# Second layer's first product by a seven-product scheme inside each block of tokens

## The chip, the cores and the metric

The kernel runs on one core of a Trainium2 chip. The metric is the device time of one execution in microseconds (us). A core has a matrix engine (TensorE, PE in the profile), three engines for elementwise work (VectorE or DVE, ScalarE or ACT, GpSimd or POOL), and a queue on SyncE (SP) from which this kernel issues all of its DMA transfers. Each engine executes its instructions in the order in which the program lists them, and waits for others by semaphores. SBUF is the working memory of 128 partitions; matmuls write into PSUM, which has eight banks of 512 float32 columns.

## The reference

Three stages follow each other; d is 512 wide, tokens are 8 x 576 = 4608.

```python
q_s = softmax(q, axis=-1); k_s = softmax(k, axis=2)
x = q_s @ (k_s^T @ v)                                   # linear attention, 8 heads of 64
x = (sigmoid(x @ w_gate) * (x @ w_val)) @ w_out         # first layer, d_ff = 1536
h = x @ w_in                                            # second layer, d_ff = 2048
P = a0 + a1*h + a2*h**2 + a3*h**3
Q = 1 + |b0|*|h| + |b1|*h**2
out = (P / (Q + 1e-6)) @ w_out2
```

Inputs of the layers' weights are 64-bit floats in the original layout, which the kernel reads as words and turns into float32 ("pieces").

## The kernel before, in words

Tokens are worked on in nine blocks of 512 columns, features in groups of 128 (f). To keep float32 precision at the matrix engine's faster rate every operand is split into a high and a low part (h, lo), and each product of two 128x128 by 128x512 tiles is three matmuls: high by high, low by high, high by low (`mm3`, lines 182 to 185). A split is two operations: ScalarE copies the value to the rounded high part (L174), and another engine subtracts it (L176, in the second layer's gates GpSimd).

The first layer works on blocks 0 to 2 one by one, and on the other six as three pairs. In a pair gate and value come from seven products (a Strassen scheme) over sums of blocks and sums of weights; summed weights are computed once, stored in DRAM (`ws_d`), and streamed back, one load of 256 KB for each product, eight products ahead (`pull`). Each pair ends with a tail of 144 matmuls (back products of its second block). During the pairs the other engines prepare what comes later: attention for the next pair, and the second layer's weights. A piece of weights (128x512) is loaded as words, put together by ScalarE and four VectorE operations (`prep_abs`, `prep_bits_a`, `prep_bits_b`, L213 to L232), split, and stored in DRAM. Ten of the 32 pieces are done in the first two pairs, 22 in the last. `pieces_at` and `PIECE_OPS` set the places of these steps in the order of the products by hand.

The second layer runs over 9 blocks x 16 groups f = 144 steps. All 32 split pieces of weights are fetched from DRAM at its start and stay in SBUF. A step has
- `front_b`: h for 128 features and 512 tokens, 4 x `mm3` = 12 matmuls of 512 columns into one PSUM bank (`ph`);
- `vec_b1`: on ScalarE Square (L1007), Abs (L1008), Identity (L1009), Ln (L1015), Exp (L1016); on VectorE L1010 to L1012. Ln and Exp give a first value of 1/Q;
- `vec_b2`, one step later: on VectorE one Newton step and the product with P (L1026 to L1028), then the split of the gate into `ghb` and `glb`;
- `back_b`, three steps after the front: 12 matmuls of 512 columns (L1039), gate by second weights, added up over f in four PSUM banks (`accb`). After f = 15 the four banks are negated to SBUF, two by ScalarE, two by VectorE (L1046, L1048), and stored.

In 16 steps the next block's x is loaded from DRAM (`x_raw`) and split, four times ScalarE and VectorE. The first three steps are interleaved with the tail of the first layer's last pair.

Of the kernel before, what the change touches and what calls it, by code (L numbers as in the profile page):

```python
# [11 lines left out]
F32 = mybir.dt.float32  # L12
# [25 lines left out]
NPROD = 7  # L38
AHEAD = 8
# [5 lines left out]
PIECE_OPS = {"early": (-5, 4, 7, 9, 10, 14), "first": (-5, 1, 2, 3, 4, 6), "second": (-2, 4, 7, 8, 9, 12)}  # L45
# [84 lines left out]
def kernel(ctx: ExitStack, tc: tile.TileContext, q, k, v, w1, w2, ab_in, out):  # L130
# [11 lines left out]
    ps_f = ctx.enter_context(tc.tile_pool(name="ps_f", bufs=2, space=PSUM))  # L142
    ps_x = ctx.enter_context(tc.tile_pool(name="ps_x", bufs=2, space=PSUM))
# [25 lines left out]
    w2_d = [dram.tile([P, 2, NB], F32, name=f"w2_{p}") for p in range(2 * NF2)]  # L169
# [28 lines left out]
    pieces += [w2[f][:, i * NB:(i + 1) * NB] for f in range(NF2) for i in range(2)]  # L198
    NW1, NW = 3 * NF1, 3 * NF1 + 2 * NF2
# [36 lines left out]
    def prep_split(p, eng=nc.gpsimd):  # L236
# [3 lines left out]
        else:  # L240
            hl = (more[0].tile([P, 2, NB], F32R, tag="hl", name="hl", bufs=2) if more else
# [4 lines left out]
    def prep_store(p):  # L246
        nc.sync.dma_start(out=w2_d[p - NW1], in_=f32(val.pop(p)))

    def fetch(p):
# [4 lines left out]
    def prep(stage_of):

        for p, n in stage_of:
            yield from (prep_load, prep_abs, prep_bits_a, prep_bits_b, prep_split, prep_store)[n](p) or ()
            yield
# [861 lines left out]
```

## Time and profile before

| | |
|---|---|
| time, median of 3 runs | 1769.9 us (1769.72 to 1772.57) |
| time of the profiled execution | 1770.29 us |
| its span, first to last instruction | 1768.5 us |
| busy: PE, PE weight load | 1727.9 us, 1413.6 us |
| busy: DVE, ACT, POOL | 1318.8, 1091.0, 449.3 us |
| mean granted TensorE clock | 0.992 of full speed |

Busy time is the sum of an engine's instructions; for the matrix engine the ends of matmuls are modelled and one reaches into the next, so the pace is read from starts. The second layer's steps begin about 958 us after the span's start and fill the rest.

### The profile page before, as it was taken

What the parts mean: (1) busy time and instruction counts of PE and PEld (TensorE: products, weight loads), DVE (VectorE), ACT (ScalarE), POOL (GpSimd) and SP (SyncE); (2) the same over time, 40 slices, a digit from 0 to 9 for tenths busy, and PEclk for the clock granted to TensorE, in tenths of its full rate; (3) what the DMA queues carried; (4) which work ended last, traced back from release to release, by engine and by line L of the source; (5) the groups of instructions that cost most, each with busy time, mean ns of one, the idle gap of its engine ahead of it and who ended that gap; (6) DMA issues with size and microseconds to landing.
All of it is one profiled execution on the core that took longest, in us unless ns stands there. A gap on an engine that the chain in (4) does not pass through costs nothing. (4 is left out here: it accounts for less than half of the span.)

```text
span 1768.5 us, 23176 instructions
## 1 busy us (share of the span) xinstructions
PE 1727.9 (98%) x8184; PEld 1413.6 (80%) x8184; DVE 1318.8 (75%) x2063; ACT 1091.0 (62%) x1790; POOL 449.3 (25%) x344
## 2 busy tenths in 40 slices
PE   5988999999999999999999999999999999999999
PEld 4767877888888888888888888888888888888887
DVE  8998787646665755677774688888788878788886
ACT  4566446555664466544444676767777777777775
POOL 2013432221113411152334222222222222222222
PEclk8999999999999999999999999999999999999999
DMA  6542865234564545638996700000000000000000
GB/s 213 178 150 75 267 229 191 63 127 154 188 234 153 200 140 200 200 126 289 346 322 224 260 24 25 24 25 24 25 24 25 24 25 24 25 24 25 1 25 24
DMA packets 112340, 217.70 MB, mean 123 GB/s; under 512 B 10848, under 2 KB 32352, under 8 KB 112224
## 3 DMA queue, kind: packets, MB, share of 16 engines
q1 hardware_dynamic: 112224, 216.22, 35.7%
q8 instruction: 65, 1.06, 0.2%
q14 instruction: 51, 0.42, 0.1%
HBM read 158.50 MB, written 57.67 MB: 122 GB/s over the span
## 5 line engine op out<-in xcount | busy, mean ns | idle before, releaser
L176 POOL TENSOR_TENSOR glb<-gb,ghb 128x512 fp32r<-128x512 f32 x144 | 187.4, 1301 | 599.0 <-ACT ghb L174 599.0
L1007 ACT ACTIVATE h<-ph 128x512 f32<-128x512 f32 x144 | 86.2, 599 | 211.6 <-PE ph L185 205.8
L1010 DVE SCALAR_TENSOR_TENSOR ah<-h,babs,ah 128x512 f32<-128x512 f32 x144 | 107.9, 749 | 76.1 <-ACT ah L1008 62.1
L1039 PE MATMUL accb<-wh,ghb 128*128 128x512 f32 x576 | 158.3, 389 | 0.0
L1039 PE MATMUL accb<-wh,glb 128*128 128x512 f32 x576 | 158.3, 389 | 0.0
L1039 PE MATMUL accb<-wl,ghb 128*128 128x512 f32 x576 | 158.3, 389 | 0.0
L1026 DVE SCALAR_TENSOR_TENSOR u<-ah,r 128x512 f32<-128x512 f32 x144 | 99.3, 689 | 40.0 <-ACT r L1016 40.0
L1039 PEld LDWEIGHTS accb<-wh,glb 128*128 128x128 f32 x576 | 108.2, 188 | 22.5
L1039 PEld LDWEIGHTS accb<-wh,ghb 128*128 128x128 f32 x576 | 108.2, 188 | 22.5
L1039 PEld LDWEIGHTS accb<-wl,ghb 128*128 128x128 f32 x576 | 108.1, 188 | 22.4
L183 PE MATMUL ph<-x_h,wh 128*128 128x512 f32 x320 | 124.5, 389 | 0.0
L184 PE MATMUL ph<-x_h,wl 128*128 128x512 f32 x320 | 124.5, 389 | 0.0
L185 PE MATMUL ph<-x_l,wh 128*128 128x512 f32 x320 | 124.5, 389 | 0.0
L1028 DVE SCALAR_TENSOR_TENSOR gb<-pp,ab,u 128x512 f32<-128x512 f32 x144 | 109.2, 758 | 16.2
L176 POOL TENSOR_TENSOR gl<-ga,gh 128x512 fp32r<-128x512 f32 x36 | 47.2, 1310 | 267.4 <-ACT gh L174 250.9
L1009 ACT ACTIVATE pp<-ph,ab 128x512 f32<-128x512 f32 x144 | 112.7, 783 | 0.0
L1012 DVE SCALAR_TENSOR_TENSOR pp<-pp,ab,ph 128x512 f32<-128x512 f32 x144 | 107.6, 747 | 5.1
L1016 ACT ACTIVATE r<-r,exp_bias 128x512 f32<-128x512 f32 x144 | 104.4, 725 | 4.7
L1015 ACT ACTIVATE r<-ah,ln_bias 128x512 f32<-128x512 f32 x144 | 104.8, 728 | 1.2 <-DVE ah L1010 0.2
L1027 DVE SCALAR_TENSOR_TENSOR u<-u,r 128x512 f32<-128x512 f32 x144 | 100.7, 699 | 4.9
L183 PE MATMUL ph<-xoh,wh 128*128 128x512 f32 x256 | 99.6, 389 | 0.0
L184 PE MATMUL ph<-xoh,wl 128*128 128x512 f32 x256 | 99.6, 389 | 0.0
(198 smaller groups left out, 4526.3 us busy)
## 6 DMA issues: line engine op xcount, KB each, us to landing
ws<-ws SPq DMA_DIRECT2D x252, 256.0 KB, 5.3
raw<-in_w SPq DMA_DIRECT2D x68, 512.0 KB, 5.2
w<-hl SPq DMA_DIRECT2D x32, 512.0 KB, 3.7
v<-in_v SPq DMA_DIRECT2D x30, 325.0 KB, 4.0
k<-in_k SPq DMA_DIRECT2D x30, 320.0 KB, 3.6
q<-in_q SPq DMA_DIRECT2D x36, 256.0 KB, 3.7
x_raw<-x SPq DMA_DIRECT2D x9, 1024.0 KB, 5.6
out<-ob SPq DMA_DIRECT2D x36, 256.0 KB, 2.3
```

What stands on the lines that cost most here:

```text
L176: lo_eng.tensor_tensor(out=lo, in0=src, in1=f32(h), op=ALU.subtract)
L183: nc.tensor.matmul(ps, wh, xh, start=first, stop=False, **kw)
L184: nc.tensor.matmul(ps, wl, xh, start=False, stop=False, **kw)
L185: nc.tensor.matmul(ps, wh, xl, start=False, stop=last, **kw)
L1009: nc.scalar.activation(pp, ph, AF.Identity, scale=ab[:, 3:4], bias=ab[:, 2:3])
L1010: nc.vector.scalar_tensor_tensor(out=ah, in0=h2, scalar=babs[:, 1:2], in1=ah, op0=ALU.mult, op1=ALU.add)
L1012: nc.vector.scalar_tensor_tensor(out=pp, in0=pp, scalar=ab[:, 1:2], in1=ph, op0=ALU.add, op1=ALU.mult)
L1015: nc.scalar.activation(r, ah, AF.Ln, scale=2.0**-LN_SHIFT, bias=ln_bias)
L1016: nc.scalar.activation(r, r, AF.Exp, scale=-1.0, bias=exp_bias)
L1027: nc.vector.scalar_tensor_tensor(out=u, in0=u, scalar=2.0, in1=r, op0=ALU.subtract, op1=ALU.mult)
L1028: nc.vector.scalar_tensor_tensor(out=g, in0=pp, scalar=ab[:, 0:1], in1=u, op0=ALU.add, op1=ALU.mult)
L1039: nc.tensor.matmul(accs["b", j][t], x[:, t * P:(t + 1) * P], y, start=(f == 0 and n == 0), stop=(f == NF2 - 1 and n == 2))
```

## The change

The second layer's steps are taken two by two (m = 0 to 7 in a block, 72 iterations i over all blocks). Inside a block the 512 tokens are two halves of 256 columns, the two groups f of an iteration are the two halves of the weights, and the 512 inputs are two halves of two 128-row tiles. Four of these 2 x 2 block products by the usual rule would be eight products; now there are seven (`product2`), each of two `mm3` of 256 columns, with weights that are sums and differences of the original ones (`wi_d`), streamed as in the first layer, and with summed inputs (`tb_all`, from `x_raw`, on ScalarE, VectorE and GpSimd) that are made one block ahead. The seven results are combined in two PSUM tiles of one bank (`px`, `py`, each with two buffers): four products add onto earlier ones in place, three copies of 256 columns go to SBUF (`s12`, `s5`), and VectorE adds them in, writing PSUM.

The elementwise chain is rewritten: Identity, Square and Abs still work on 512 columns (half k of an iteration: one f). Ln and Exp on ScalarE and five `scalar_tensor_tensor` on VectorE work on 1024 at once: `vec_ah` and `vec_pp` (h squared times a coefficient, added to ah and pp), `vec_u1` and `vec_u2` (ah with r, the Newton step) and `vec_g` (pp times ah). The two products of pp with `ps` (`vec_p2`) and the splits (`vec_split`: L174 on ScalarE, L176 on GpSimd) are of 512 columns. It is written as small functions that `close(n)`, after product n, calls for this iteration or an earlier one (`VEC`: function, lag in iterations). `back_b` is emitted some matmuls at a time after each product (`BACK_SHARE`), three iterations behind the front.

Preparation: all 16 pieces of the second weights are done in the first two pairs (eight each); the last pair does the 16 pieces of the first weights and the sums (`sums2_*`). Only the second weights are fetched to stay (`outs`), 32 tiles. The tail of the last pair (`tail_all`) is spread over the making of block 0's summed inputs (48 matmuls) and the first three iterations. The shares of back matmuls after the first layer's products are altered, and an exhausted one no longer uses up a count.

```diff
+EARLY = 16
+PIECE_OPS = (-5, 4, 7, 9, 10, 14)
+PAIR_OPS = (
+    ((-6, 1, 2, 3), (-2, 4, 7, 8), (9, 10, 11, 13, 5, 6, 11, 12, 13, 14)),
+    ((5, 11, 14, 15), (9, 13, 16, 17), (18, 20, 21, 22, 16, 17, 20, 21, 22, 23)))
+BACK_SHARE = (3, 3, 4, 3, 4, 4, 3)
...
+    def sums2_a(p):
+        a, b = val[p], val[p + 1]
+        t = more[0].tile([P, 4, 2 * P], F32, tag="st", name="st", bufs=1)
+        sums2[p] = [t]
+        nc.vector.tensor_tensor(out=t[:, 1], in0=b[:, :2 * P], in1=b[:, 2 * P:], op=ALU.add)
+        nc.vector.tensor_tensor(out=t[:, 2], in0=a[:, :2 * P], in1=b[:, :2 * P], op=ALU.subtract)
+    def sums2_b(p):
+        a, t = val[p], sums2[p][0]
+        nc.vector.tensor_tensor(out=t[:, 0], in0=t[:, 1], in1=a[:, :2 * P], op=ALU.subtract)
+        nc.vector.tensor_tensor(out=t[:, 3], in0=a[:, 2 * P:], in1=t[:, 0], op=ALU.subtract)
+    def sums2_c(p):
+        h = stage.tile([P, 4, 2 * P], F32R, tag="raw", name="sh")
+        sums2[p].append(h)
+        nc.scalar.activation(h, sums2[p][0], AF.Copy)
+    def sums2_d(p):
+        t, h = sums2[p]
+        nc.vector.tensor_tensor(out=t.bitcast(F32R), in0=t, in1=f32(h), op=ALU.subtract)
...
-            share = (1, 2, 2, 1, 2, 2, 2)
+            share = (0, 2, 2, 2, 2, 2, 2)
...
+    def tb_split(j, n, src, eng):
...
+        nc.scalar.activation(h, src, AF.Copy)
+        yield
+        eng.tensor_tensor(out=lo, in0=src, in1=f32(h), op=ALU.subtract)
+        yield
...
+    def tb_all(j):
+        b11, b12, b21, b22 = (quarter(k, t) for k in range(2) for t in range(2))
+        t = wnew(F32, "tr").rearrange("p (c t) -> p c t", t=HB)
+        yield from tb_split(j, 0, b11, nc.vector)
+        nc.gpsimd.tensor_tensor(out=t, in0=b12, in1=b11, op=ALU.subtract)
+        yield
+        yield from tb_split(j, 1, b21, nc.vector)
+        yield from tb_split(j, 3, t, nc.vector)
+        nc.gpsimd.tensor_tensor(out=t, in0=b22, in1=t, op=ALU.subtract)
+        yield
+        yield from tb_split(j, 5, b22, nc.vector)
+        nc.gpsimd.tensor_tensor(out=b12, in0=b22, in1=b12, op=ALU.subtract)
+        yield
+        yield from tb_split(j, 2, t, nc.vector)
+        nc.gpsimd.tensor_tensor(out=t, in0=b21, in1=t, op=ALU.subtract)
+        yield
+        yield from tb_split(j, 4, b12, nc.vector)
+        yield from tb_split(j, 6, t, nc.vector)
...
+    def product2(i, n, ps):
+        t = stream.pop((i, n))
+        for c in range(2):
+            h, lo = (t[:, k * 2 * P + c * P:k * 2 * P + (c + 1) * P] for k in range(2))
+            th, tl = TB[i // NM, n]
+            mm3(ps, h, lo, th[:, c, :], tl[:, c, :], n in (0, 1, 3) and c == 0, c == 1, skip_group_check=True)
...
+    def vec_pp(i):
+        ps, ah, pp, r = vb[i]
+        nc.vector.scalar_tensor_tensor(out=pp, in0=r, scalar=ab[:, 3:4], in1=pp, op0=ALU.mult, op1=ALU.add)
+    def vec_ah(i):
+        ps, ah, pp, r = vb[i]
+        nc.vector.scalar_tensor_tensor(out=ah, in0=r, scalar=babs[:, 1:2], in1=ah, op0=ALU.mult, op1=ALU.add)
+    def vec_p2(i, k):
+        ps, ah, pp, r = vb[i]
+        nc.vector.tensor_tensor(out=pp[:, k], in0=pp[:, k], in1=ps[k], op=ALU.mult)
...
+    VEC = (
+        ((vec_g, 2), (on(1, vec_id), 1)), ((on(1, vec_sq), 1), (on(1, vec_abs), 1), (vec_ah, 1), (on(0, vec_split), 2)),
+        ((vec_pp, 1), (on(1, vec_split), 2)), ((vec_ln, 1), (on(0, vec_p2), 1)),
+        ((vec_exp, 1), ), ((on(1, vec_p2), 1), (vec_u1, 1), (on(0, vec_id), 0)),
+        ((vec_u2, 1), (on(0, vec_sq), 0), (on(0, vec_abs), 0)))
...
+        def close(n):
+            vec(i, n)
+            if 1 <= m < NM - 1 and n in (1, 3, 5):
+                next(building, None)
...
+            back_some(share[n])
+            if n in (1, 3, 5):
+                fetch_some()
+            pull2(i * NPROD + n + 1 + AHEAD)
...
+        product2(i, 0, yl)
+        nc.scalar.activation(s12[:, :HB], yl, AF.Copy)
+        close(0)
+        product2(i, 1, xl)
+        close(1)
+        product2(i, 2, yl)
+        nc.scalar.activation(s12[:, HB:], yl, AF.Copy)
+        close(2)
+        product2(i, 3, xr)
+        nc.scalar.activation(s5, xr, AF.Copy)
+        close(3)
+        product2(i, 4, yl)
+        nc.vector.tensor_tensor(out=yr, in0=yl, in1=s5, op=ALU.add)
+        close(4)
+        product2(i, 5, xr)
+        nc.vector.tensor_tensor(out=ps[0], in0=ps[0], in1=s12, op=ALU.add)
+        close(5)
+        product2(i, 6, yl)
+        close(6)
```

Here xl, xr are the halves of `px` and yl, yr those of `py`. In the text below ah, pp, u1, u2 and g are VectorE's 1024-column operations of these names, "low part" is GpSimd's L176 in `vec_split`, and building is `tb_all` for the next block, three of its steps in each iteration with m = 1 to 6.

## Rows read from the trace of the kernel before

**Rows 1.** The page's busy time, its share and the instructions by engine.
```profile
PE 1727.9 (98%) x8184; PEld 1413.6 (80%) x8184; DVE 1318.8 (75%) x2063; ACT 1091.0 (62%) x1790; POOL 449.3 (25%) x344
```
**Rows 2.** Busy time by stretch: last pair, second layer (columns are named).
```profile
core 0: us, PE busy (x) PEld busy (x) DVE busy (x) ACT busy (x) POOL busy (x), PEclk, DMA share, GB/s
801.00:945.00 144.00, 143.84 (x635) 118.75 (x634) 107.97 (x150) 71.92 (x123) 49.03 (x36) 1.00 0.86 300
1164.00:1700.00 536.00, 536.00 (x2367) 443.81 (x2366) 436.45 (x630) 388.37 (x629) 128.18 (x99) 1.00 0.07 24
```
**Rows 3.** TensorE in order of time: start, duration, engine, line, operation.
```profile
333.89 0.28 PE L183 MATMUL ps_xt<-qh,kvh 128*128 128x256 f32 x1
...
334.61 0.39 PE L183 MATMUL pg<-x_h,wh 128*128 128x512 f32 x1
```
**Rows 4.** The same view: a front's last matmul and ScalarE after it.
```profile
1503.22 0.39 PE L185 MATMUL ph<-x_l,wh 128*128 128x512 f32 x1
1503.65 0.60 ACT L1007 ACTIVATE h<-ph 128x512 f32<-128x512 f32 x1 [1.71 <-PE ph L185]
...
1504.71 0.79 ACT L1009 ACTIVATE pp<-ph,ab 128x512 f32<-128x512 f32 x1
1505.38 0.64 ACT L174 ACTIVATE ghb<-gb 128x512 fp32r<-128x512 f32 x1
1505.89 0.73 ACT L1015 ACTIVATE r<-ah,ln_bias 128x512 f32<-128x512 f32 x1
```
**Rows 5.** ScalarE's groups by shape: count, busy us, mean ns, idle before.
```profile
L422 ACT ACTIVATE xs<-ps_xt 128x256 f32<-128x256 f32 x8 | 2.9, 384 | 7.0 <-PE ps_xt L185 7.0
L422 ACT ACTIVATE xs<-ps_xt 128x512 f32<-128x512 f32 x4 | 2.4, 598 | 0.4 <-PE ps_xt L185 0.2
```
**Rows 6.** VectorE in order of time, one step of the second layer.
```profile
1504.86 0.75 DVE L1010 SCALAR_TENSOR_TENSOR ah<-h,babs,ah 128x512 f32<-128x512 f32 x1 [0.60 <-ACT ah L1008]
1505.53 0.69 DVE L1011 TENSOR_TENSOR pp<-pp,ph 128x512 f32<-128x512 f32 x1
1506.25 0.75 DVE L1012 SCALAR_TENSOR_TENSOR pp<-pp,ab,ph 128x512 f32<-128x512 f32 x1
...
1508.14 0.69 DVE L1027 SCALAR_TENSOR_TENSOR u<-u,r 128x512 f32<-128x512 f32 x1
1508.95 0.75 DVE L1028 SCALAR_TENSOR_TENSOR gb<-pp,ab,u 128x512 f32<-128x512 f32 x1
```
**Rows 7.** Single lines of VectorE: duration ns minimum/median/maximum, first and last start.
```profile
L692 DVE TENSOR_TENSOR sl<-st,sh x12: 1210/1220/2571, 176.7 to 287.3; 128x1024 fp32r<-128x1024 f32 x12
L676 DVE TENSOR_TENSOR st<-sr x12: 410/418/421, 170.6 to 275.9; 128x256 f32<-128x256 f32 x12
```
**Rows 8.** VectorE and GpSimd in order of time, two places.
```profile
580.44 0.68 DVE L722 TENSOR_TENSOR tl<-tr,th 128x512 fp32r<-128x512 f32 x1
580.46 1.82 POOL L176 TENSOR_TENSOR bl<-vb,bh 128x512 fp32r<-128x512 f32 x1 [1.82 <-ACT bh L174]
581.04 1.79 DVE L745 TENSOR_TENSOR xs<-xs 128x512 f32<-128x512 f32 x1
...
589.55 1.77 DVE L722 TENSOR_TENSOR tl<-x_raw,th 128x512 fp32r<-128x512 f32 x1
...
1506.09 1.30 POOL L176 TENSOR_TENSOR glb<-gb,ghb 128x512 fp32r<-128x512 f32 x1 [4.14 <-ACT ghb L174]
```
**Rows 9.** The gate's product on VectorE: minimum/median/maximum ns.
```profile
L1028 DVE SCALAR_TENSOR_TENSOR gb<-pp,ab,u x144: 751/752/1659, 968.4 to 1759.2; 128x512 f32<-128x512 f32 x144
```
**Rows 10.** TensorE in order of time, its last matmul.
```profile
1764.37 0.39 PE L1039 MATMUL accb<-wh,glb 128*128 128x512 f32 x1
```
**Rows 11.** Busy time on the tile val in the last pair: DVE, ACT, POOL.
```profile
801.00:945.00 144.00, 68.86 (x88) 27.15 (x44) 31.72 (x22) 1.00 0.86 300
```
**Rows 12.** DMA issues: count, KB each, median us from issue to landing.
```profile
ws<-ws SPq DMA_DIRECT2D x252, 256.0 KB, 5.3
```
**Rows 13.** TensorE's weight loads by shape: count, busy us, mean ns, idle.
```profile
L1039 PEld LDWEIGHTS accb<-wh,glb 128*128 128x128 f32 x576 | 108.2, 188 | 22.5
```

More of the change, by code (lines that the diff above doesn't have):

```diff
@@ L26 @@
 NB = 512
+HB = NB // 2
 NBLK = NT // NB
 NF1, NF2 = F1 // P, F2 // P
+NM = NF2 // 2
 KC = DM // P
@@ L830, in back_some @@
     def back_some(n):
-        for _ in range(n):
-            if not backs:
-                return
+        while n and backs:
             if next(backs[0], backs) is backs:
                 backs.pop(0)
+            else:
+                n -= 1
     def back_all():
@@ L936 @@
         T.clear()
+        if last:
+            for f in range(NF1):
+                do(("t", s, f))
         back_all()
@@ L939 @@
         back_list.clear()
-        if last:
-            split_x()
         back_all()
@@ L957, with tail_all @@
         run(building)
-    def fetch_some(spare):
-        while len(wt) < NW and live[0] + 2 + spare <= 6 * NF1:
-            live[0] += 2
-            fetch(len(wt))
-    def tail_some(a, b):
-        for f in range(a, b):
+    front_ctx.close()
+    ps_w = ctx.enter_context(tc.tile_pool(name="ps_w", bufs=2, space=PSUM))
+    def tail_all():
+        for f in range(NF1):
             if f + 2 < NF1:
                 split_held(f + 2, nc.gpsimd)
-            run(tail(PAIRS - 1, f))
-            fetch_some(4 if f < NF1 - 1 else 0)
-    fetch_some(4)
-    tail_some(0, 4)
+            yield from tail(PAIRS - 1, f)
     more_ctx.close()
@@ L1000 @@
[L1000 to L1014 removed]
+    TB = {}
@@ new lines, in vec, with fetch_some @@
+    def vec(i, n):
+        for fn, lag in VEC[n]:
+            if 0 <= i - lag < NBLK * NM:
+                fn(i - lag)
+    def fetch_some():
+        gates = sum(x[0] == "b" for x in g_t)
+        later = 8 - 2 * gates + 15 - sum(x[0] == 1 for x in TB) * 2
+        if len(outs) < NF2 and live[0] + 2 + later <= 6 * NF1:
+            live[0] += 2
+            fetch(len(outs))
+    stream.clear()
+    building = tb_all(0)
+    backs.append(tail_all())
+    for n in range(4 * 12):
+        back_some(1)
+        if n % 2 == 0:
+            next(building, None)
@@ L1081, in _layout @@
+    assert len(outs) == NF2
+    for i in range(NBLK * NM, NBLK * NM + 3):
+        for n in range(NPROD):
+            vec(i, n)
+        for k in range(2):
+            run(back_b(i - 3, k))
 def _layout(i):
```

238 lines of the change are left out of this document (137 added, 101 removed).

## The prediction

> **What bounds the kernel now.** I read the busy totals first, then busy time by stretch, then the order in time of the second layer's step. TensorE is busy 1727.9 of 1768.5 us [rows 1]. In the stretch from 1164 to 1700 us, all second layer, it is busy for all 536 us at full granted clock, while VectorE has 436, ScalarE 388 and GpSimd 128 us [rows 2]. So only TensorE's matmul time counts there, as long as nobody makes it wait. These 536 us hold 2367 matmuls of 512 columns, 226.5 ns each; a step (one f of one block, 144 in all) has 24 and takes 5.44 us.
>
> **TensorE, what is removed.** Two steps become one iteration (72, m = 0 to 7 in each block). The back stays 24 matmuls of 512 columns, 5.44 us. The front goes from as many to 7 products of 6 matmuls of 256. Matmuls of 256 columns stand in the trace six in a row: from the first start to the next matmul 0.72 us in three of four such runs and 0.71 in one [rows 3], 119.6 ns each. Front: 42 x 0.1196 = 5.02 us instead of 24 x 0.2265 = 5.436, so 0.413 us saved, 72 x 0.413 = 29.7 us in all. An iteration is 10.46 us, a product 0.718.
> The Trainium skill ("TensorE: Matmul & The Clock Gate", Back-to-back issue gap) gives an isolated gap of N/2.4 + 2.5 ns; by it a front would go from 24 x 215.8 to 42 x 109.2 ns, saving 0.59 us and 43 us in all. The rows show about 11 ns more per matmul at both widths, and there are 18 more of them, so the rows' figure is taken.
>
> **ScalarE** (starts in time order [rows 4]): Square and Abs 1.06 together, Identity to the next 0.67, a copy 0.51 us. A copy of 512 columns takes 598 ns, of 256 columns 384 [rows 5], so 512 columns more cost 0.43, and Ln and Exp at 1024 columns 0.73 + 0.43 = 1.16 each. Three copies of 256 columns come in, 0.27 each start to start (an operation overlaps the next by 0.11). Sum 0.81 + 2 x (1.06 + 0.67 + 0.51) + 2.3 = 7.6 us, 8.1 with one split copy of the next block's summed inputs: it has over 2 us free.
>
> **VectorE, per iteration.** Start to start [rows 6]: an operation that doesn't need the one before takes its duration less 0.08 (L1010 to L1011), one that does its duration plus 0.03 (L1011 to L1012). Going from 512 to 1024 columns adds 0.53 us (1220 ns [rows 7] against 0.69 us). So u1 1.25, u2 1.29 (a wait for two semaphores, L1027 to L1028, costs some more), g 1.20, ah 1.20, pp 1.31; two vec_p2, each 0.605; the in-place add into px 0.605; the 256-column add into yr 0.34 (418 ns [rows 7]). Sum 8.4 us of 10.46: alone it fits.
>
> **The price: GpSimd's subtractions stop VectorE.** At 580 us GpSimd's L176 comes while VectorE works on a subtraction with both inputs in SBUF, waits for its end, and then VectorE's next such operation lasts 1.79 us instead of 0.68; from then on the two alternate, VectorE's starts 1.70 us apart (five intervals from 581.04 to 589.55) [rows 8]. 1.70 less the 0.605 between two such starts undisturbed (580.44 to 581.04) is 1.09 us lost for each GpSimd operation that lands between two of VectorE's. A scalar_tensor_tensor is stopped alike: L1028 takes 752 ns in the median and 1659 at most [rows 9]. With an operand in PSUM it isn't: L1012 ran 0.75 us inside GpSimd's 1.30 us [rows 6, 8]. Before, that was GpSimd's only partner. After, all five 1024-column operations have both inputs in SBUF, and vec_split follows ah and pp.
> The Trainium skill says so of the chip ("SBUF — State Buffer", Terms: the port pair of VectorE and GpSimd is held for a whole instruction and the loser blocks; "Advanced Engine Details and Errata", GPSIMD Details: it conflicts with two SBUF inputs). The trace agrees, 1.79 against 0.68 us. By the rule alone an iteration loses up to 2.2 us and never less where no PSUM operand lies beside.
>
> Clock of an iteration, 0 at product 0: products start at 0, 1.40, 2.80, 4.42, 5.82, 7.44, 9.07, the backs lie between. ScalarE starts 0.20 us after a product's end (1503.65 against the last start of 1503.22 plus 0.227 [rows 4]). Its copy of yl at 0.92, Identity, Square and Abs of half 1 end at 3.03; ah starts at 3.07. The gate's low part (L176) is waiting by 3.7, so it takes 1.09 us between ah and pp; vec_p2 follows at 6.67, the add into yr at 7.28, and the second low part runs beside these two PSUM operations, free. Product 6 needs yr's add done by 9.07, so yr may start as late as 8.60. Iterations without building (m = 0, 7, and all of the last block) lose nothing.
> With tb_all running, VectorE also has a split of 0.605. At m = 1 and 2 it falls behind vec_p2, waits for the second low part, and yr is at 8.4 and 8.5: the reserve is gone. At m = 2 two output copies (0.605 each) follow, so at m = 3 ah starts at 4.26. From m = 3 to 6 the split stands between ah and pp, and both low parts are caught: 8.4 + 0.605 + 2 x 1.09 = 11.19 us per iteration. At m = 3 yr starts at 4.26 + 1.20 + 1.09 + 0.605 + 1.09 + 1.31 + 0.605 = 10.16 and ends, with the handover, at 10.63: product 6 waits 1.56 us. At m = 4, 5, 6 the wait is 11.19 - 10.46 = 0.73. Sum 3.75 us per block, for blocks 1 to 7 26.3; in block 0, where the first layer's rest lengthens the first three iterations, 0.37 + 2.19 = 2.6. Together 28.8 us; the last block builds nothing.
> Ends: with no second low part caught, 4 us; with ah waiting for ScalarE (0.15, a split copy stands ahead) and four of the ten operations 0.09 longer for a second semaphore (L1027 to L1028), 32 x 0.51 = 16 more, 45 us. Adds that write into PSUM stand nowhere in the trace: nearest is the product that reads PSUM, 0.69 us (L1011 [rows 6]); taken at that, kept from -10% to +50%.
>
> **Edges.** At the end the last gate comes later after its product: counted from the last front's iteration end, ah at 2.85, the low part, pp, two vec_p2, u1 at 7.7, u2, g and the copy put its high part at 12.25 us, while the 48 back matmuls before it cover 10.88: +1.4 us. Before, the backs ran on without a gap to their last start at 1764.37 us [rows 10]. At the start, the first layer's rest (144 matmuls) still covers the first split and the first three fronts: 0, bounds -1 to +5.
> Last pair of the first layer: 22 prepared pieces become 16, with eight sets of sums. VectorE per piece 68.86/22 = 3.13 us [rows 11]; sums 4 x 0.42 + 1.22 = 2.9. So 68.9 becomes 50.1 + 23.2 = 73.3 us, 112 of 144 us busy instead of 108 [rows 2]. ScalarE, 27.2/44 = 0.62 each [rows 11], goes from 44 such to 24, 8 half as wide (0.4) and 8 twice (1.05): 26.5; GpSimd, 31.7/22 = 1.44, to 8 and 8 half: 17. On SP 22 loads and 22 stores become 16 and 48 smaller, all behind each other on one queue. All of it lies beside products that keep TensorE full: 0, bounds -0.2 to +8. The first two pairs get three more pieces each: 0 to +2. The 64 weight loads at the second layer's start become 32. The altered share of the backs moves nothing while TensorE is full.
> Stream: 504 loads of 256 KB, one per 1.49 us, 176 GB/s. The same load landed in 5.3 us [rows 12], eight are ahead (11.9 us), and in the last pair 300 GB/s left TensorE 143.84 of 144 us busy [rows 2]. SP's output stores, which wait for their copies, stand in front of loads once per block; the lead covers 6.6 us. Cost 0, bounds 0 to +10.
>
> Sum against the profiled execution, 1770.3 us (span 1768.5; the median of the runs is 0.4 lower): 1770.3 - 29.7 + 28.8 + 1.4 = 1770.8.
>
> **Rivals.**
> 1. TensorE keeps the lead: of the two low parts at m = 3 to 6 only one stops VectorE. Then 10.10 us fit in 10.46 and only m = 3 waits, 0.5 us: 1770.3 - 29.7 + 4 + 1.4 = 1746; with none caught 1742. For it: GpSimd is free for most of each iteration. Against: in the alternation no waiting operation was passed over [rows 8].
> 2. Slower: the two adds that write PSUM cost half again as much, 0.5 us per iteration on VectorE's path. It decides from 0.1 us on, since m = 3 to 6 have no reserve: 4 x 0.5 + 1 (m = 1, 2) = 3 us per block, 24 in all: 1794. For it: no row shows VectorE writing PSUM. Against: reading PSUM costs nothing (0.69 us, L1011 and L1027 alike [rows 6]).
> 3. Preparation or stream late: the sums' bursts hold up the first layer's additions, or loads miss the lead: +8 to +18, 1778 to 1788.
> 4. The change doesn't give its saving: in a long run of 256-column matmuls the weight loads, 188 ns each [rows 13], set the pace: 42 x 0.188 + 5.44 = 13.3 us per iteration, 72 x (13.3 - 10.87) = +175: 1945. Against: the six in a row ran at 119.6.
>
> **How the numbers follow.** Forecast 0.50 (own range 1757 to 1785: waits of 15 to 43 us); rival 1 0.25; rival 2 0.12; rival 3 0.10; rival 4 0.03. A measurement tells about 0.2%, 3.5 us. The forecast's half divides into 0.16 faster, 0.18 same, 0.16 slower; rival 1 is faster, 2 to 4 slower but for 0.02. Faster 0.41, same 0.20, slower 0.39. Range 1743 to 1796: it takes in rival 1 but for its end, and rivals 2 and 3.
>
> **What would show it.** Right: TensorE waiting for VectorE's add into yr, at m = 3 to 6 only, near 0.7 us each, and ah or pp lasting 2.4 us beside L176. Matmuls of 256 columns 120 ns apart. Wrong: TensorE busy throughout at 10.46 us per iteration (rival 1); waits in the last block too, or the in-place adds above 0.8 us (rival 2); waits for wi or in the last pair (rival 3); 188 ns apart (rival 4).

## The result, and the profile after

The changed kernel takes 1794.0 us (median of 4 runs, 1792.37 to 1797.03) against 1770.0 before: ratio 1.0134 [1.0117, 1.0152], 1.3% slower. The prediction said 1770.8, no change, with 1743 to 1796 as its range and 1757 to 1785 as the forecast's own. The profiled execution's span is 1792.0 us.

Two lines of the page answer to [rows 1]: busy time by engine, and the costliest new group.

```profile
PE 1715.8 (96%) x9480; PEld 1444.8 (81%) x9480; DVE 1470.3 (82%) x1914; ACT 1130.3 (63%) x1897; POOL 604.5 (34%) x380
...
L1106 DVE SCALAR_TENSOR_TENSOR pp<-r,ab,pp 128x1024 f32<-128x1024 f32 x72 | 165.5, 2299 | 0.0
```

TensorE's work did shrink, by 12 us; the span grew by 23.5. So TensorE, idle 41 us in 1768.5 before, is now idle 76 us. Busy time by stretch, the same two as in [rows 2], says where:

```profile
801.00:945.00 144.00, 142.81 (x628) 117.25 (x627) 107.63 (x158) 64.51 (x110) 33.70 (x26) 1.00 0.86 290
...
1164.00:1700.00 536.00, 515.70 (x3200) 457.67 (x3199) 511.64 (x490) 405.67 (x686) 230.65 (x121) 1.00 0.58 188
```

In the second layer TensorE, full before, has 20 us of gaps at full granted clock, and VectorE has gone from 436 to 512 of 536 us. What TensorE waits for from 970 us to the end (the view of waits: who, line, waited for: us in total, times, longest):

```profile
PE py L192 <- DVE py L1236: 28.3, 25, 1.2
PE accb L1150 <- ACT gh L183: 2.2, 1, 2.2
PE py L192 <- ACT s L1225: 0.8, 1, 0.8
```

L1236 is the add into yr, the wait that the prediction named. Its 25 rows stand at m = 4, 5 and 6 of each of the eight building blocks, and in block 0 at m = 3 too, 1.13 us on average, and nowhere in the last block. VectorE in order of time through one such iteration (start, duration, line; in brackets idle time before and what ended it), to be read beside [rows 6, 8]:

```profile
1379.19 2.31 DVE L1106 SCALAR_TENSOR_TENSOR pp<-r,ab,pp 128x1024 f32<-128x1024 f32 x1
1381.53 0.69 DVE L1114 TENSOR_TENSOR pp<-pp,px 128x512 f32<-128x512 f32 x1
1382.14 0.43 DVE L1236 TENSOR_TENSOR py<-py,s 128x256 f32<-128x256 f32 x1
1382.47 0.69 DVE L1239 TENSOR_TENSOR px<-px,s 128x512 f32<-128x512 f32 x1
1383.07 0.68 DVE L1114 TENSOR_TENSOR pp<-pp,py 128x512 f32<-128x512 f32 x1
1383.96 1.23 DVE L1126 SCALAR_TENSOR_TENSOR ah<-ah,r 128x1024 f32<-128x1024 f32 x1 [0.21 <-ACT r L1122]
1385.22 1.22 DVE L1130 SCALAR_TENSOR_TENSOR ah<-ah,r 128x1024 f32<-128x1024 f32 x1
1386.48 1.28 DVE L1134 SCALAR_TENSOR_TENSOR pp<-pp,ab,ah 128x1024 f32<-128x1024 f32 x1
1388.21 1.28 DVE L1110 SCALAR_TENSOR_TENSOR ah<-r,babs,ah 128x1024 f32<-128x1024 f32 x1 [0.45 <-ACT ah L1102]
1389.41 1.78 DVE L1046 TENSOR_TENSOR tl<-tr,th 128x512 fp32r<-128x512 f32 x1
1391.11 2.31 DVE L1106 SCALAR_TENSOR_TENSOR pp<-r,ab,pp 128x1024 f32<-128x1024 f32 x1
```

From one L1106 to the next is 11.92 us. The split of the next block (L1046) and pp (L1106) take 1.78 and 2.31 us. In the kernel of the first experiment, where GpSimd has no part in the gate, they take 0.68 and 1.28. So each is stopped once, for 1.10 and 1.03 us, by a low part on GpSimd (gl, L185); the prediction had 1.09. GpSimd's two low parts lie beside them, one after the other, 3.57 us instead of two times 1.30:

```profile
1388.78 3.57 POOL L185 TENSOR_TENSOR gl<-pp,gh 128x512 fp32r<-128x512 f32 x2 [6.15 <-ACT gh L183]
```

The two waits in brackets of VectorE's rows were not in the forecast; its upper end had 0.15 us for the second. ScalarE in the same iteration shows where they come from:

```profile
1381.59 1.15 ACT L1118 ACTIVATE r<-ah,ln_bias 128x1024 f32<-128x1024 f32 x1 [3.65 <-DVE pp L1106]
1382.77 1.15 ACT L1122 ACTIVATE r<-r,exp_bias 128x1024 f32<-128x1024 f32 x1
...
1387.46 0.72 ACT L1102 ACTIVATE ah<-py,babs 128x512 f32<-128x512 f32 x1
```

Ln needs ah, which ends 1.62 us before the next pp starts (1388.21 + 1.28 against 1391.11; an iteration earlier that is 1377.6), but it starts at 1381.59, when pp has ended. The reason is in the code: `vec_ln` writes its result into r, the tile that holds the squares, and `vec_pp` still reads r. So a stopped pp holds up Ln, Ln holds up Exp, u1 (L1126) waits 0.21 us for Exp, and the ScalarE work queued behind Exp makes ah wait 0.45 us for Abs. Over the 72 iterations Ln waits 156.3 us for pp, in 70 rows.

The time from one start of the yr add to the next is the length of an iteration, named by the m that it leads into: in a building block (the fourth, m = 0 to 7) 9.72, 11.03, 10.54, 10.94, 11.93, 11.93, 11.93 and 10.55 us, in sum 88.57; in the last block, which builds nothing, a plain iteration is 10.54.

### The profile page after: what moved, and what is told of

The parts are those of the page before. It is cut to its first block, busy times and chain, and to the rows that moved or that the text cites. A ratio compares the mean times of both kernels' runs of the same rounds, so it can differ in the third digit from the quotient of the medians.

```text
span 1792.0 us, 27297 instructions
## 1 busy us (share of the span) xinstructions
PE 1715.8 (96%) x9480; PEld 1444.8 (81%) x9480; DVE 1470.3 (82%) x1914; ACT 1130.3 (63%) x1897; POOL 604.5 (34%) x380
## 4 chain that ended last, share of the span: by engine, by line
PE 63%; DVE 17%; ACT 9%; issue 6%; DMA 3%; POOL 1%; SPq 0%; ACTq 0%; DVEq 0%; POOLq 0%
PE accb L1150 13%; PE acc L477 13%; DVE pp L1106 3%; PE pa L192 3%; PE pa L193 3%; PE pa L194 3%; PE py L192 3%; PE py L193 2%; PE py L194 2%; DMA wi<-wi 2%; PE px L193 2%; PE px L194 2%; PE px L192 2%; DVE tl L1046 2%; ACT pp L1094 2%
## 5 line engine op out<-in xcount | busy, mean ns | idle before, releaser
L185 POOL TENSOR_TENSOR gl<-pp,gh 128x512 fp32r<-128x512 f32 x144 | 275.7, 1935 | 456.0 <-ACT gh L183 299.8
L1150 PE MATMUL accb<-wh,gh 128*128 128x512 f32 x576 | 185.3, 394 | 2.5 <-ACT gh L183 2.2
L1150 PE MATMUL accb<-wl,gh 128*128 128x512 f32 x576 | 185.6, 395 | 0.0
L1150 PE MATMUL accb<-wh,gl 128*128 128x512 f32 x576 | 185.0, 394 | 0.0
L1118 ACT ACTIVATE r<-ah,ln_bias 128x1024 f32<-128x1024 f32 x72 | 82.9, 1151 | 156.3 <-DVE pp L1106 156.3
L1106 DVE SCALAR_TENSOR_TENSOR pp<-r,ab,pp 128x1024 f32<-128x1024 f32 x72 | 165.5, 2299 | 0.0
L192 PE MATMUL py<-th,wi 128*128 128x256 f32 x416 | 118.3, 284 | 14.8 <-DVE py L1236 13.5
L185 POOL TENSOR_TENSOR gl<-ga,gh 128x512 fp32r<-128x512 f32 x36 | 51.3, 1425 | 226.2 <-ACT gh L183 226.0
L194 PE MATMUL py<-tl,wi 128*128 128x256 f32 x416 | 117.3, 282 | 0.0
L193 PE MATMUL py<-th,wi 128*128 128x256 f32 x416 | 117.1, 281 | 0.0
L1150 PEld LDWEIGHTS accb<-wh,gh 128*128 128x128 f32 x576 | 100.4, 189 | 13.1 <-ACT gh L183 2.7
L1150 PEld LDWEIGHTS accb<-wl,gh 128*128 128x128 f32 x576 | 100.5, 189 | 10.1
L1126 DVE SCALAR_TENSOR_TENSOR ah<-ah,r 128x1024 f32<-128x1024 f32 x72 | 88.0, 1222 | 12.9 <-ACT r L1122 12.7
L185 POOL TENSOR_TENSOR hl<-val,hl 128x512 fp32r<-128x512 f32 (+1 forms) x32 | 38.2, 1194 | 171.0 <-ACT hl L183 84.2
L1130 DVE SCALAR_TENSOR_TENSOR ah<-ah,r 128x1024 f32<-128x1024 f32 x72 | 89.0, 1236 | 1.9
```

The source lines that it names most:

```text
L185: lo_eng.tensor_tensor(out=lo, in0=src, in1=f32(h), op=ALU.subtract)
L192: nc.tensor.matmul(ps, wh, xh, start=first, stop=False, **kw)
L193: nc.tensor.matmul(ps, wl, xh, start=False, stop=False, **kw)
L194: nc.tensor.matmul(ps, wh, xl, start=False, stop=last, **kw)
L1106: nc.vector.scalar_tensor_tensor(out=pp, in0=r, scalar=ab[:, 3:4], in1=pp, op0=ALU.mult, op1=ALU.add)
L1126: nc.vector.scalar_tensor_tensor(out=ah, in0=ah, scalar=q_one, in1=r, op0=ALU.add, op1=ALU.mult)
```

## The experiments

Changed lines are shown against the kernel after, except where it says before. Times of the profiled execution are compared by span (1792.0 after). Where no ratio is given, the time is that of one execution.

**The low part on VectorE.** GpSimd is taken out of the gate; VectorE gets two operations of 0.69 us more per iteration.

```diff
-        split(h, lo, g, nc.gpsimd)
+        split(h, lo, g, nc.vector)
```


> The gates' low parts (two subtractions of 512 columns per iteration) go from GpSimd to VectorE; nothing else is altered. Theory A, VectorE loses 1.09 us to each GpSimd subtraction that lands between two of its own with both inputs in SBUF: doing the two itself costs 2 x 0.605 us, being stopped by them 2 x 1.09, so the iterations with building at m = 4 to 6 fall from 11.93 to 8.4 + 0.6 + 1.2 + 0.2 = 10.4 to 10.6 us, where TensorE sets the pace (10.54), and the time to 1755 to 1762 us. Rival B, VectorE simply has too much work and it is all one where the subtraction runs: 1.2 us more in each such iteration, 13.1 us, and 1825 to 1835 us in all.

Measured 1766.7 us, ratio to before 0.9981 [0.9972, 0.9991]: 27 us less than after, with more work on the engine that is late. The time moved as theory A had it, and ended 5 us above its range; rival B is out. So the stops are the main cause. VectorE in order of time here:

```profile
1384.17 0.69 DVE L185 TENSOR_TENSOR gl<-pp,gh 128x512 fp32r<-128x512 f32 x1
1384.77 0.68 DVE L1046 TENSOR_TENSOR tl<-x_raw,th 128x512 fp32r<-128x512 f32 x1
1385.37 1.28 DVE L1106 SCALAR_TENSOR_TENSOR pp<-r,ab,pp 128x1024 f32<-128x1024 f32 x1
1386.57 0.69 DVE L185 TENSOR_TENSOR gl<-pp,gh 128x512 fp32r<-128x512 f32 x1
```

Two low parts cost VectorE 1.2 us of its own time instead of 2.1 us of stops, and pp is early enough that Ln waits 80.8 us instead of 156.3. TensorE still waits for yr once per block, at m = 5, 0.58 us. Blocks 1 to 7 take 85.2 us on average. VectorE is busy 521 of 536 us. The one wait per block is a stop too: just ahead of it the second low part (L185, now on VectorE) lasts 1.79 us instead of 0.69, beside a subtraction that GpSimd still does for the next block's sums (L1063); rows of it are shown with the three cures.

**A tile of its own for Ln and Exp.** GpSimd stays in the gate; only the overwritten tile goes.

```diff
+        q_t[i] = tb.tile([P, 2, NB], F32, tag="q", name="q", bufs=1)
...
-        nc.scalar.activation(r, ah, AF.Ln, scale=2.0**-LN_SHIFT, bias=ln_bias)
+        nc.scalar.activation(q_t[i], ah, AF.Ln, scale=2.0**-LN_SHIFT, bias=ln_bias)
...
```
(Exp, u1 and u2 read and write q in the same way.)

> Ln and Exp write a tile of their own (q) instead of r, which vec_pp still reads. Theory C, Ln waits for pp only because it overwrites r, and that lateness comes back as u1 waiting for Exp (0.21 us) and ah for Abs (0.45): with its own tile both waits go, iterations m = 4 to 6 fall from 11.93 to about 11.3, and the time by 14 to 20 us to 1774 to 1780. Rival D, the waits only show slack that VectorE loses to GpSimd anyway, and ScalarE is late by its own load: iterations stay at 11.8 to 11.93, 1790 to 1794 us.

Measured 1779.5 us, ratio to before 1.0057 [1.0038, 1.0075]: 14.5 us less than after, as theory C had it. Iterations at m = 4 to 6 go from 11.93 to 11.39 us, and TensorE's waits for yr (the same view) from 28.3 to 15.4:

```profile
PE py L192 <- DVE py L1237: 15.4, 25, 1.2
```

11.39 is near the 11.19 that the prediction had for two stops without these waits; u1's wait is gone, and of ah's 0.20 us are left. So the loss at m = 4 to 6 has two parts: 0.54 us from the overwritten tile, the rest from the stops.

**No stream.** The first eight loads of summed weights are used again and again, for all later products too.

```diff
+            if len(fixed) < AHEAD:
+                fixed.append(wnew(F32R, "wi"))
...
+            stream[i, n] = fixed[ahead2[0] % AHEAD]
```


> The second layer's stream of summed weights is left out: after the first eight loads their tiles are used again and again (the weights are wrong from there on). The back matmuls of 512 columns start 233 ns apart in the changed kernel, 226.5 before. Theory E, the stream's 180 GB/s into SBUF slows them: they return to 226.5, undisturbed iterations from 10.54 to 10.38, time 1782 to 1784. Rival F, the mixture with matmuls of 256 columns does it: 233 ns and 10.54 stay, time 1792 to 1795.

Measured 1792.9 us, the cycles of 10.54 and 11.93 unchanged: theory E falls, rival F holds. The stream costs nothing that shows, and the plain iteration's 0.08 us above the prediction isn't its doing.

**Fronts of 256 columns in the kernel before.** Each front matmul is split into two of 256 columns (the second half's start discards the first half's sums, so h is incomplete).

```diff
-            mm3(ph, wh[:, s], wl[:, s], xh, xl, kk == 0, kk == KC - 1)
+            for c in (slice(0, NB // 2), slice(NB // 2, NB)):
+                mm3(ph[:, c], wh[:, s], wl[:, s], xh[:, c], xl[:, c], kk == 0, kk == KC - 1, skip_group_check=True)
```


> The kernel before, with each front matmul of 512 columns split into two of 256 (24 instead of 12 per step, same values). By the 119.6 ns of the rows before and 226.5 for the back: a step 24 x 0.1196 + 12 x 0.2265 = 5.59 us instead of 5.44, 144 x 0.15 = +22 us, 1792. Theory F, backs beside 256-column matmuls take 233 ns: step 24 x 0.118 + 12 x 0.2333 = 5.63, 1797 us. Theory E, only the stream slows them, which is not here: backs at 226.5 and 24 x 0.118: 5.55, 1786.

1795.4 us (span 1793.6), a step 5.61 us instead of 5.44: above theory E's 1786 us, which falls, and between the 1792 of undisturbed widths and theory F's 1797. TensorE in order of time (starts and counts; a row of x4 is four matmuls):

```profile
1500.54 0.28 PE L183 MATMUL ph<-xoh,wh 128*128 128x256 f32 x1
...
1503.41 1.09 PE L1040 MATMUL accb<-wh,ghb 128*128 128x512 f32 x4
1504.34 1.07 PE L1040 MATMUL accb<-wl,ghb 128*128 128x512 f32 x4
1505.25 1.07 PE L1040 MATMUL accb<-wh,glb 128*128 128x512 f32 x4
```

24 matmuls of 256 columns take 2.87 us, 119.6 ns each as in [rows 3]. The first four of 512 columns behind them take 0.93 us, the next four 0.91 (0.906 at 226.5 ns each). So a run of 512-column matmuls behind narrow ones pays some 0.02 us once, and not in each matmul as theory F had it.

**Fewer runs of back matmuls.** If each run pays, four runs should save against seven.

```diff
-BACK_SHARE = (3, 3, 4, 3, 4, 4, 3)
+BACK_SHARE = (6, 0, 6, 0, 6, 6, 0)
```


> The same 24 back matmuls of an iteration stand in four runs of 6 instead of seven of 3 or 4. Switch theory: each change from a run of 256-column matmuls to one of 512 columns costs some 0.02 to 0.025 us, so three fewer save 0.06 to 0.075 us per iteration: in the last block, where nothing makes TensorE wait, the cycle goes from 10.54 to about 10.47 us, in all 72 iterations 4 to 5 us if no new wait comes. Rival: the back matmuls are slower one by one (233 instead of 226.5 ns each, for their operands or their bank), so that the cycle stays at 10.54 us whatever the runs.

The plain iteration is 10.55 to 10.57 us, not 10.47: the switch theory's forecast fails, and its rival's comes in (whether for its reason, the next run tells). The kernel takes 1804.4 us, because the iteration into m = 3 grows from 10.94 to 12.47 and TensorE waits for the yr add there too, in every building block. TensorE in order of time, one run of each width (a run ends where the next row starts):

```profile
1736.35 1.09 PE L1150 MATMUL accb<-wh,gh 128*128 128x512 f32 x4
1737.28 0.62 PE L1150 MATMUL accb<-wl,gh 128*128 128x512 f32 x2
1737.74 0.28 PE L192 MATMUL px<-th,wi 128*128 128x256 f32 x1
...
1739.17 0.63 PE L1150 MATMUL accb<-wl,gh 128*128 128x512 f32 x2
```

Six of 512 columns: 1.39 us, 0.03 above 6 x 0.2265. Twelve of 256: 1.43, nearly 12 x 0.1196.

**Two runs of 12.** The lengths of single runs are read here.

```diff
-BACK_SHARE = (3, 3, 4, 3, 4, 4, 3)
+BACK_SHARE = (12, 0, 0, 0, 12, 0, 0)
```


> Only the share of the back matmuls is changed, to two runs of 12. What is read is the length of the runs, not the time. In four runs of 6 each took 1.385 to 1.39 us, in seven of 3 or 4 0.70 and 0.93, where 226.5 ns each would give 1.36, 0.68 and 0.906. If each run pays once, 0.02 to 0.03 us, a run of 12 takes 2.74 us; if each matmul beside 256-column fronts is slower, 0.2315, it takes 2.78. The time itself is worse than before the edit: the front's last products stand close together, and VectorE's adds between them are waited for: 1800 to 1830 us.

One run in TensorE's order of time, as above:

```profile
1786.75 1.09 PE L1150 MATMUL accb<-wh,gh 128*128 128x512 f32 x4
1787.68 1.07 PE L1150 MATMUL accb<-wl,gh 128*128 128x512 f32 x4
1788.59 1.07 PE L1150 MATMUL accb<-wh,gl 128*128 128x512 f32 x4
1789.49 0.28 PE L192 MATMUL px<-th,wi 128*128 128x256 f32 x1
```

2.74 us here and 2.75 on average of eleven between 1730 and 1800 us, not 2.78: each run pays once, 0.02 to 0.03 us, and the rival's reason is out. (The time, 1835.8 us, is above its range: with no backs between them products wait for one another, 68 times, 34.6 us.) Why seven runs cost no more than four is seen in the kernel after, in a plain iteration of the last block:

```profile
1733.90 0.28 PE L192 MATMUL px<-x_h,wi 128*128 128x256 f32 x1
...
1734.61 0.86 PE L1150 MATMUL accb<-wl,gh 128*128 128x512 f32 x3
1735.31 0.39 PE L1150 MATMUL accb<-wh,gl 128*128 128x512 f32 x1
1735.53 0.28 PE L192 MATMUL py<-x_h,wi 128*128 128x256 f32 x1
```

Six of 256 columns take 0.71 us, 0.01 less than 6 x 0.1196; four of 512 take 0.92, 0.01 to 0.02 more than at 226.5 ns. A short narrow run gives back nearly half of what the wide run behind it pays; a narrow run of 12 (1.43) gives back hardly anything. Seven pairs of short runs and four pairs of longer ones come out alike, 10.54 and 10.56. What in the engine makes it so was not found.

**The first layer's share.** Undoing the new share of the backs among a pair's products.

```diff
-            share = (0, 2, 2, 2, 2, 2, 2)
+            share = (1, 2, 2, 1, 2, 2, 2)
```


> The first layer's share of back matmuls goes from (0,2,2,2,2,2,2) back to (1,2,2,1,2,2,2). After the change the three pairs take 167.5, 160.2 and 144.1 us from their first to their last pa product, 5.2, 4.7 and 4.9 us more than before. Theory G: part of that comes from the share. With no back matmul behind pa and two behind the fourth product, pb starts about 0.2 us earlier after VectorE's L979 and waits for it (rows of 0.3 to 0.5 us, each costing about twice that). Then the pb waits go, each pair is 1 to 1.5 us shorter, and the kernel takes about 1790 us. Rival H: the share moves nothing, the waits are VectorE being late by its added work; then the pairs keep their lengths within 0.3 us and the kernel stays at 1793 to 1794 us.

Both theories are wrong: 1803.3 us (span 1800.5), 8.5 longer. From the first to the last matmul into pa the three pairs take 169.5, 163.9 and 144.2 us, against 168.0, 160.6 and 144.5 after: 4.4 us in sum. Of the rest, 2.0 lie ahead of the first pair, and in the drain, behind a wait of 2.23 us, eight matmuls run 427 ns apart at a granted clock of 0.50 (the 1.2 GHz level), which costs 1.6 us and did not happen in the profiled execution of the kernel after. The waits for pb do vanish, but a worse one comes (TensorE's waits from 399 to 960 us):

```profile
PE acc L477 <- ACT gh L183: 9.1, 9, 1.5
```

With one matmul behind pa, it belongs to a gate whose high part is not yet copied. The new share avoids that; undoing it does not shorten the pairs.

**Less VectorE work in the first two pairs.**

```diff
-            at(t + m, fn, NW1 + n)
+            if n % 8 > 2 or fn not in (prep_bits_a, prep_bits_b):
+                at(t + m, fn, NW1 + n)
```


> The two bit operations of VectorE are left out for three of the eight prepared pieces in each of the first two pairs (the three more per pair that the change brought), so these weights are not rounded as they should be. Theory H: what VectorE got more to do in the pairs is what lengthens them. Three pieces have two such operations of some 0.5 us each, so VectorE is spared about 3 us per pair; if the waits for ga (rows of 0.65 us, three in pair 1, each costing about twice that) go, pairs 1 and 2 are 2 to 4 us shorter, the third pair stays at 144.1, and the kernel takes 1787 to 1791 us. Rival G (the share of the backs): the pairs stay at 167.5 and 160.2 us within 0.5 us.

1790.7 us; pairs 1 and 2 take 166.0 and 159.4 us, 2.0 and 1.3 shorter. Three of the four waits of pc in these pairs go. So theory H holds in its direction and for the time, and misses for pair 2 (2 to 4 us were forecast). The edit takes away more than the expectation says: `prep_bits_a` and `prep_bits_b` are two operations each, so four per piece, and VectorE's busy time from 395 to 805 us falls by 17 us, from 286.0 to 268.7. All of that gives 3 us, so most of it had cost TensorE nothing. Where it did cost, is seen in VectorE's order of time in the kernel after:

```profile
488.57 0.99 DVE L230 TENSOR_SCALAR val<-val 128x512 f32<-128x512 f32 x1
489.59 0.43 DVE L233 TENSOR_SCALAR val<-val 128x512 uint32<-128x512 uint32 x1
490.05 0.69 DVE L952 TENSOR_TENSOR ga<-pb,s 128x512 f32<-128x512 f32 x1
```

and in TensorE's row behind it:

```profile
490.80 0.50 PE L192 MATMUL pc<-th,ws 128*128 128x512 f32 x1 [0.67 <-DVE ga L952]
```

The two operations (both of `prep_bits_a`) stand ahead of the add that frees pb's bank, and pc waits for it. The first takes 0.99 us where 0.42 is its median (34 of them, in val). GpSimd has begun a product of its own (L350) beside it:

```profile
487.70 1.57 POOL L350 TENSOR_TENSOR k<-k,kma 128x640 f32<-128x640 f32 x1
```

At the two other waits of pc in pair 1 (506 and 522 us) L230 takes 0.93 us, again beside L350. So 0.5 to 0.6 us of these waits of 0.63 to 0.67 is VectorE lengthened beside GpSimd, as in the second layer, and not its own work.

**Cures together, with long runs.** Low parts on VectorE (placed behind product 4), the own tile, four runs of backs, and the first layer's rest spread over the first three iterations.

```diff
-BACK_SHARE = (3, 3, 4, 3, 4, 4, 3)
+BACK_SHARE = (6, 0, 6, 0, 6, 6, 0)
...
-        split(h, lo, g, nc.gpsimd)
+        nc.scalar.activation(h, g, AF.Copy)
...
-        share = BACK_SHARE if i > 2 else (5, ) * 7
+        share = BACK_SHARE if i > 2 else (5, 5, 5, 4, 5, 4, 4)
```


> Three cures together: both gate subtractions on VectorE (GpSimd no longer stops it), Ln and Exp in a tile of their own (Ln no longer waits for pp), and the backs in four runs of 6, in the first three iterations (5,5,5,4,5,4,4) with the tail. If the three causes are the whole of the second layer's loss, VectorE's work per building iteration (8.4 us, two subtractions of 0.605, a split of 0.605, in sum 10.2) fits the 10.47 us of TensorE, a building block takes about 84 us as the last one does, against 85.2 with the first cure alone and 88.6 with none, and the kernel takes 1750 to 1758 us, faster than before by 0.7 to 1.1%. If the first cure's 1766.7 us is limited by the sum of VectorE's work itself (waits of 11.5 us cycles stay), it stays at 1763 to 1768 us.

1767.2 us, ratio 0.9984 [0.9975, 0.9994]: no better than the first cure alone. Blocks take 85.3 and 86.3 us in turn, and TensorE waits 1.06 to 1.21 us once per block, now between the yr adds of m = 3 and 4. A stop stands ahead of these waits as well: in every building block one low part, at m = 3 to 4, lasts 1.78 us instead of 0.69 beside GpSimd's L1060, a subtraction for the next block's sums. That it falls where it costs this much may be due to the runs of 6 (in their own experiment they lengthened the iteration into m = 3 by 1.5 us) or to the changed place of the low parts; the two were not separated.

**Three cures that leave TensorE's order alone.**

```diff
-PIECE_OPS = (-5, 4, 7, 9, 10, 14)
+PIECE_OPS = (-5, 4, 8, 9, 10, 14)
...
-        split(h, lo, g, nc.gpsimd)
+        split(h, lo, g, nc.vector)
```
(and the own tile as above)

> Three cures that don't touch the order of TensorE's work: the gate's low parts on VectorE, Ln and Exp in a tile of their own, and in the first two pairs the first two bit operations of a prepared piece one product later, so that they stand behind the addition of pb (L952) instead of ahead of it. Theory: with the low parts alone on VectorE, TensorE still waits 0.58 us for the add into yr once per block (at m = 5), each some 1.2 us in the cycle, and the pairs take 167.7 and 160.4 us. The own tile takes the once-per-block waits away (about 8 us over seven blocks), the moved bit operations the three waits for ga in pair 1 and some in pair 2 (2 to 3 us): 1766.7 less 7 to 11, 1756 to 1760 us. Rival: VectorE's work itself (some 10.2 us in a building iteration, with what it loses between operations that need each other) is too near to the 10.54 us of an iteration; the waits stay, and only the pairs gain: 1763 to 1766 us.

1758.3 us (5 runs), ratio to before 0.9937 [0.9924, 0.9951]. The first two pairs take 165.1 and 159.1 us, 2.8 and 1.5 less: one number in a table of places gives 4 us, more than leaving that work out for three pieces in eight. One product later L230 takes 0.41 us at these places: the move takes it out of the add's way and away from GpSimd's L350 at once, and the two were not separated. The own tile adds less than the theory had: the wait at m = 5 shrinks from 0.58 to 0.27 us and doesn't go; from the first to the last add into yr it is 759.9 us against 762.1. Alone the tile gave 14.5 us; beside the first cure, some 3 with the drain (its wait goes from 1.80 to 1.04 us). What is left at m = 5 is not VectorE's own work, as the rival had it, but one more stop. VectorE and GpSimd in order of time:

```profile
1454.59 2.21 POOL L1063 TENSOR_TENSOR tr<-x_raw,tr 128x512 f32<-128x512 f32 x1 [16.48 <-ACT s L1234]
...
1455.56 1.79 DVE L185 TENSOR_TENSOR gl<-pp,gh 128x512 fp32r<-128x512 f32 x1
```

The same low part takes 0.69 us an iteration earlier. It is stopped so ahead of each of the once-per-block waits, in this kernel and in the first experiment's. The cure that suggests itself, this subtraction on VectorE or at another place, was not tried.

**And the rest of the first layer spread** (on top of the three cures).

```diff
-        share = BACK_SHARE if i > 2 else (5, ) * 7
+        share = BACK_SHARE if i > 2 else (5, 5, 5, 4, 5, 4, 4)
```


> The same as the kernel with the three cures, and the first layer's rest spread over the first three iterations as (5,5,5,4,5,4,4) instead of 5 behind each product. Theory: the third iteration of block 0 now has 35 matmuls of the rest as well, instead of 26 with the last front products bare, so the waits of 1.22 and 0.45 us at 1015 and 1037 us go: 1 to 3 us less than the kernel with the three cures, 1753 to 1759 us. Rival: the waits move to the next iteration and the time is the same within 1 us.

1755.5 us (5 runs, 1755.08 to 1756.55), ratio to before 0.9926 [0.9913, 0.9938]: the fastest version, 0.7% below the kernel before and clear of noise (by the two ratios to before, 0.9926/1.0134 = 0.979 of the time after). The wait of 1.22 us is gone, and with it a stopped low part ahead of it (at 1009.58 us in the kernel with the three cures), so the spread's share in it is not separate from the stop's. What TensorE still waits for from 970 us on:

```profile
PE py L192 <- DVE py L1237: 1.8, 7, 0.3
PE accb L1151 <- ACT gh L183: 1.0, 1, 1.0
PE accb L1151 <- ACT xo L488: 0.4, 1, 0.4
```

The seven waits for yr stand in blocks 0 and 2 to 7. In block 1 the low part (L185) is not stopped, and there TensorE does not wait: in this one kernel, with and without the stop side by side, the wait comes and goes with it.

## Why the prediction was right or wrong

**The mechanism held in the main.** TensorE's wait stands where it was put, at the add into yr in building blocks, caused by GpSimd's low parts stopping VectorE by 1.09 us (1.03 and 1.10 measured). It stands at m = 4 to 6 and not at m = 3, and its size needed a second wait that the prediction didn't have (below). The first experiment shows it by taking the cause away. The Trainium skill ("Advanced Engine Details and Errata", GPSIMD Details) says that GpSimd conflicts with VectorE's operations on two SBUF inputs; L1106 at 2.31 against 1.28 us agrees.

The measured time is outside the forecast's own range, 1757 to 1785. It is inside the wide one only because that took in rivals 2 and 3, and rival 2's 1794 is met by luck.

**What failed was the sizes around it**, in all 1794.1 (the profiled execution) less 1770.8, 23.3 us. The terms, as near as the rows tell:

| term | forecast | measured | difference |
|---|---|---|---|
| first two pairs ("0 to +2") | 0 | about +5.5 | +5.5 |
| last pair ("0, bounds -0.2 to +8") | 0 | about +2.8 | +2.8 |
| plain iteration | 10.46 us | 10.54 us | 72 x 0.08 = +5.8 |
| blocks 1 to 7, excess over 8 plain iterations | 3.75 each | 88.57 - 84.32 = 4.25 | +3.5 |
| block 0 | 2.6 | about 7 | +4.4 |
| start and drain | 1.4 | rows of 2.24 and 0.75 us | some +2 |

- **"The first two pairs get three more pieces each: 0 to +2"** and, of the last pair, **"All of it lies beside products that keep TensorE full: 0"** cost most together. From the first to the last matmul into pa the three pairs and what lies between take 10.5 us more (399.2 to 949.1, against 400.5 to 939.9). About 2.5 of it are back matmuls that moved from behind a pair into it (a step of seven products has 54 matmuls instead of 53, 12.24 instead of 12.01 us, and the stretches between pairs are 2 us shorter). The rest, 8 us, is TensorE's waits: eleven rows of 0.2 to 0.9 us, 5.9 in all, eight of them in the first two pairs, where before there were three with 1.0 (VectorE ends ten of the eleven). With the 0.25 to 0.3 us more that each costs (below) this is 8.9 less 1.8; rows of 0.1 us make up the rest. Room in VectorE's busy time was taken to be enough; the place of each operation in VectorE's order, and GpSimd beside it, was not looked at.
- **"An iteration is 10.46 us"**: both widths were taken from undisturbed rows. Beside each other, 24 wide matmuls take 5.57 instead of 5.44 us and 42 narrow ones 4.97 instead of 5.02 (means over the last block). The saving is 72 x (10.873 - 10.54) = 24 us, not 29.7.
- **"8.4 + 0.605 + 2 x 1.09 = 11.19 us per iteration"** was 11.93. The sum counted VectorE's operations and not ScalarE's wait for a tile that VectorE still reads. 11.39 without that wait (second experiment) shows the sum itself was within 0.2. The other end cancels most of it: at m = 3, where both low parts were to be caught and TensorE to wait 1.56 us, only one is (the split L1046 takes 0.68 us there, pp 2.31), the yr add comes 0.4 us later than the pace, and TensorE doesn't wait. So 3.75 and 4.25 us are near each other by luck, for two errors that cancel.
- **Block 0**: in the third iteration the first layer's rest runs out (26 instead of 35 of its matmuls), VectorE's output copies come, and the iteration into m = 3 takes 13.83 us; then three at 11.93. Six rows of waiting with 5.4 us, and what each costs beyond its row, make the 7. The same eight iterations take 96.2 us here and 90.0 in the last experiment, which itself has two short waits there (0.41 and 0.16 us).
- **The drain**: the wait for the last gate's high part is 2.24 us instead of 1.4. It falls to 0.99 with the own tile and to 1.80 with the low parts on VectorE, so the late Ln is the larger part.
- **Each wait costs more than its row**: with one wait of 0.58 us (first experiment) a block takes 85.16 us, with one of 0.27 (three cures) 84.87, and eight plain iterations are 84.32. So a row of waiting costs itself and 0.25 to 0.3 us more. Starts show where this lies, at the wait at 1382.62 us with its row of 1.12: it starts 1.51 us after the matmul before, 0.23 being the pace, so 1.28 us are lost, 0.16 more than the row, which counts only from the modelled end; the next start comes 0.22 us later instead of 0.12.

**The rivals.** Rival 1 (TensorE keeps the lead) did not happen: in 71 of the 72 iterations, all but the first, pp is stopped (2.31 us or more), and at m = 4 to 6 the split too. With the low parts taken off GpSimd by hand the time is 1766.7 and not 1742 to 1746, for the first layer's 8, the width's 5.8, block 0, the drain and a wait per block. Rival 2 priced adds into PSUM half as much again; they cost what was assumed, 690 and 424 ns for 512 and 256 columns, so its 1794 came about by other causes. Rival 3 was half right: the preparation is late, the loads never (4.7 us to land, no wait for them, and no change without them). Rival 4 falls: narrow matmuls run 118 to 120 ns apart in runs of 6 and of 12.

## What to carry to other kernels

A share of 75% on a helper engine doesn't say that an edit there is free: look at what stands just ahead of the operation that frees the busy engine's bank, and at what GpSimd does beside it. When an operation writes its result over its input's neighbour, list who else still reads that tile; such a wait stays hidden until the reader is slowed, and then it adds to the loss (here 0.54 us to 0.85 in an iteration). Work that GpSimd shares with VectorE through SBUF can be dearer than doing it on VectorE: here 1.03 to 1.10 us of stop against 0.6 us of work.

## What the runs showed of the hardware that was not expected

- TensorE behind a change from 256 to 512 columns pays 0.02 to 0.03 us once per run (2.75 us for 12, 1.39 for 6, 0.93 for 4, where 226.5 ns each give 2.72, 1.36 and 0.91), and short narrow runs give some of it back (0.71 us for 6 instead of 0.718).
- A wait of TensorE costs 0.25 to 0.3 us beyond the row that shows it, 0.16 of it because the row counts from a modelled end, 0.1 in the first matmul behind it.
- GpSimd's half of the conflict: its subtraction of 128x512 lasts 1.93 us on average in the gate (L185, 144 of them), against 1.30 beside an operation of VectorE that reads PSUM [rows 8].
- A VectorE operation that reads a single tile was lengthened beside GpSimd too: L230, a tensor_scalar of 128x512, took 0.93 to 0.99 us beside GpSimd's L350, 0.42 in the median.
